# Batch 0 of a fused linear attention and GELU MLP: both transposes first, both kv next, both x in one stretch

## The chip, the cores and the metric

The kernel runs on one core of one Trainium2 chip. The metric is the device time of one execution in microseconds (us), as a median of several runs. Most executions of one kernel lie within about 0.3 us of each other here, so a difference of 0.1 us between two medians means little by itself. What happens inside is read from the profile of one execution, whose times count from the start of its span. PE is the matrix engine TensorE, PEld its weight loads, DVE is VectorE, ACT is ScalarE, POOL is GpSimd, SPq and ACTq are the queues that issue DMAs.

## The reference, cut to what matters

```python
q_s = softmax(q over head_dim)          # 8 batches, 8 heads, 576 positions, 64
k_s = softmax(k over positions)
kv  = einsum('bhsd,bhse->bhde', k_s, v)
x   = einsum('bhsd,bhde->bhse', q_s, kv)      # -> 4608 tokens of 512
out = gelu(x @ w_in) @ w_out                  # 512 -> 2048 -> 512
```

(Shortened: the softmaxes are written out in the original.) The second part is nearly all of the arithmetic. The first part must be done for batch 0 before it can start, and for the other batches it is woven into the second part of the batch before.

## The kernel before

Batch 0 goes through these helpers. `half` 0 is heads 0 to 3, `half` 1 heads 4 to 7. `tp` transposes q, `kv` multiplies exp(k) with v, `x` multiplies transposed q with normalised kv, and `h_phase` is the first matrix multiplication with its GELU.

```python
def kv_norm(b, half=None): ...   # VectorE: reciprocal and multiplication, from PSUM
def tp_mm(b, half): ...          # PE: eight 128x128 transposes into one PSUM tile
def tp_evac(b, half, eng="v"):   # copy of that tile to SBUF
    ...
def x_evac(b, hp, eng="v"): ...  # copy of one x tile, 128x512, to SBUF

def cast_wi(i, w, eng):          # f32 -> bf16 of piece i of w_in
    ...
    if eng == "p":
        for h in range(2):
            nc.gpsimd.tensor_copy(out=o[:, 2 * h:2 * h + 2], in_=w[:, 2 * h:2 * h + 2])
    else:
        for c in range(NDM):
            nc.vector.tensor_copy(out=o[:, c], in_=w[:, c])
```

The order of batch 0, as issued:

```python
    exp_q(0, parts=2); exp_k(0, parts=2)
    norm_q(0, 0, 2)                  # multiplication on GpSimd
    norm_q(0, 1, 2, nc.vector)       # multiplication on VectorE
    tp_mm(0, 0)
    cast_v(0, 0, nc.scalar); cast_v(0, 1, nc.scalar)
    tp_evac(0, 0, "s")
    warm(1)
    cast_v(0, 2, nc.gpsimd); cast_v(0, 3, nc.gpsimd)
    ...
    kv_mm(0, 0); kv_norm(0, 0)
    tp_mm(0, 1); tp_evac(0, 1)
    x_mm(0, 0);  x_evac(0, 0, "s")
    cast_wi_dm(0, wi[0], 0, nc.scalar)
    for dm in range(1, NDM):
        cast_wi_dm(0, wi[0], dm, nc.gpsimd)
    kv_mm(0, 1); kv_norm(0, 1)
    x_evac(0, 1)
    x_mm(0, 1);  x_evac(0, 2, "s"); x_evac(0, 3)
    cast_wi(1, wi[1], "p")           # the second piece of w_in, on GpSimd, in two casts
    table(AF.Gelu)
    h_phase(0, {0: [lambda: cast_wi(2, wi[2], "v")], ...}, groups={0: 2, 4: 4, 8: 4}, ...)
```

(Calls are joined on one line and tile allocations are left out.) The groups of `h_phase` mean: column blocks 0 and 1 of the hidden layer run together, four matmuls each, then block 2, then block 3. Blocks 2 and 3 use the second piece of w_in.

The softmax here doesn't subtract the row's maximum and nothing guards it: scores larger than these inputs give would overflow.

Of the kernel before, what the change touches and what calls it, by code (L numbers as in the profile page):

```python
# [16 lines left out]
def kernel(  # L17
# [16 lines left out]
    nc = tc.nc  # L34
# [7 lines left out]
    NDM = DM // 128  # L42
# [10 lines left out]
    psum_h = ctx.enter_context(tc.tile_pool(name="psum_h", bufs=3, space=bass.MemoryType.PSUM))  # L53
    psum_y = ctx.enter_context(tc.tile_pool(name="psum_y", bufs=2, space=bass.MemoryType.PSUM))
    psum_a = ctx.enter_context(tc.tile_pool(name="psum_a", bufs=1, space=bass.MemoryType.PSUM))
# [100 lines left out]
    def cast_v(b, hp, eng=nc.vector):  # L156
        o = v_aug[b % 2][:, hp, :, 0:D]
        i = st[b]["vf"][:, hp, :].rearrange("p (n d) -> p n d", n=NS)
        if eng is nc.scalar:
            eng.copy(out=o, in_=i)  # L160
        else:
            eng.tensor_copy(out=o, in_=i)  # L162
# [5 lines left out]
    def kv_tiles(b):  # L168


        if b == 0:
            p = [psum_h.tile([128, 512], FP32, tag="h", name="kv")[:, 0:256] for i in range(2)]
            ps = psum_a.tile([128, 4, 256], FP32, tag="a2", name="kv")
            st[b]["kvall"] = ps[:, 0::2]
            p += [ps[:, 0, :], ps[:, 2, :]]
        else:
            ps = psum_a.tile([128, 4, 256], FP32, tag="a2", name="kv")
            st[b]["kvall"] = ps
            p = [ps[:, i, :] for i in place]
        st[b]["kv"] = p  # L180
# [7 lines left out]
    def kv_mm(b, half):  # L188


        if "kv" not in st[b]:
            kv_tiles(b)
        for n in range(NS):
            for i in range(2):
                for hh in range(2):
                    hp = 2 * half + i
                    pr = slice(hh * 64, hh * 64 + 64)
                    c = slice((hh ^ i) * 64, (hh ^ i) * 64 + 64)
                    nc.tensor.matmul(  # L199
                        st[b]["kv"][hp][c, 0:D + 1], ek[b % 2][pr, hp, n, :],  # L200
                        v_aug[b % 2][pr, hp, n, 0:D + 1], start=(n == 0), stop=(n == NS - 1),
                    )

    def kv_norm(b, half=None):

        ps = st[b]["kvall"]
        if half is None:
            parts = [(ps, kvc[b], 4)]
        elif b == 0 and half == 0:
            parts = [(st[b]["kv"][hp].unsqueeze(1), kvc[b][:, hp:hp + 1], 1) for hp in range(2)]  # L210
        elif b == 0:
            parts = [(ps, kvc[b][:, 2:4], 2)]
        else:
            parts = [(ps[:, 1:3] if half == 0 else ps[:, 0::3], kvc[b][:, 2 * half:2 * half + 2], 2)]
        for src, dst, m in parts:
            rec = small.tile([128, 4], FP32, tag="reck")
            nc.vector.reciprocal(rec[:, 0:m], src[:, :, D])
            nc.vector.tensor_tensor(  # L218
                out=dst, in0=src[:, :, 0:D],
                in1=rec[:, 0:m].unsqueeze(2).to_broadcast([128, m, D]), op=ALU.mult,  # L220
            )
# [21 lines left out]
    def tp_mm(b, half):  # L243
        if half == 0:
            st[b]["qT"] = attn_sb.tile([128, J, HP, 128], BF16, tag="qT", name="qT")
        if b == 1 and half == 1:
            ps = psum_a.tile([128, 2, J, 2, 128], BF16, tag="a2", name="tp")[:, 0]
        else:
            pool, tag = (psum_h, "h") if half == 1 else (psum_a, "a")
            ps = pool.tile([128, J, 2, 128], BF16, tag=tag)  # L250
        st[b][f"tp{half}"] = ps
        for i in range(2):
            hp = 2 * half + i
            for j in range(J):
                nc.tensor.transpose(  # L255
                    ps[:, j, i, :],
                    st[b]["eq"][:, j, 2 * hp:2 * hp + 2, :].rearrange("p h d -> p (h d)"),
                    identity,
                )

    def tp_evac(b, half, eng="v"):
        o = st[b]["qT"][:, :, 2 * half:2 * half + 2, :]
        if eng == "v":
            nc.vector.tensor_copy(out=o, in_=st[b][f"tp{half}"])
        else:
            nc.scalar.copy(out=o, in_=st[b][f"tp{half}"])
# [12 lines left out]
    def x_tile(b, hp, pool, tag):  # L279
        if "xT" not in st[b]:  # L280
            st[b]["xT"] = attn_sb.tile([128, HP, M], BF16, tag="xT", name="xT")
        st[b][f"x{hp}"] = pool.tile([128, M], FP32, tag=tag, name="ps")

    def x_mm(b, half):

        for bb in range(B if b == B else 1):
            for r in range(2):
                for i in range(2):
                    hp = 2 * half + i
                    pr = slice(r * 64, r * 64 + 64)  # L290
                    c = slice((r ^ i) * 64, (r ^ i) * 64 + 64)
                    ps = st[b][f"x{hp}"]
                    if b < B:
                        nc.tensor.matmul(  # L294
                            ps[c, :], kvc_of(b, hp)[pr], st[b]["qT"][pr, :, hp, :],
                            start=True, stop=True,
                        )
                    else:
                        nc.tensor.matmul(  # L299
                            ps[c, bb * R:(bb + 1) * R], kvc_of(bb, hp)[pr],  # L300
                            st[b]["qT"][pr, bb // 2, hp, bb % 2 * R:(bb % 2 + 1) * R],
                            start=True, stop=True,
                        )

    def x_all(b):

        for hp in range(HP):
            pool, tag = (psum_h, "h") if hp < 3 else (psum_a, "a")
            x_tile(b, hp, pool, tag)
        x_mm(b, 0)  # L310
        x_mm(b, 1)
        for hp, eng in ((0, "s"), (2, "v"), (1, "s"), (3, "v")):
            x_evac(b, hp, eng)

    def x_evac(b, hp, eng="v"):
        ps = st[b][f"x{hp}"]
        if eng == "v":
            nc.vector.tensor_copy(out=st[b]["xT"][:, hp, :], in_=ps)  # L318
        else:
            nc.scalar.copy(out=st[b]["xT"][:, hp, :], in_=ps)  # L320
# [88 lines left out]
    def load_wi(i):  # L409

        w = wst.tile([128, NDM, 512], FP32, tag="w")
        n = wi_cols[i]
        src = moe_w_in[:, wi_off[i]:wi_off[i] + n].rearrange("(c p) f -> p c f", p=128)
        d = NDM // wi_parts[i]
        for c in range(0, NDM, d):
            nc.sync.dma_start(out=w[:, c:c + d, 0:n], in_=src[:, c:c + d])
        return w
# [15 lines left out]
    def cast_wi_dm(i, w, dm, eng):  # L433

        n = wi_cols[i]
        r = n // 128
        o = wi_bf[:, dm, wi_off[i]:wi_off[i] + n].rearrange("p (c m) -> p c m", c=r)
        w = w[:, dm, 0:n].rearrange("p (m c) -> p c m", c=r)
        if eng is nc.scalar:
            eng.copy(out=o, in_=w)  # L440
        else:
            eng.tensor_copy(out=o, in_=w)

    def load_wo(i):
        w = wst.tile([128, 4, DM], FP32, tag="w")
# [26 lines left out]
    def warm(n, z=zeros):  # L472
        ps = psum_y.tile([128, DM], FP32, tag="y")
        for i in range(n):
            nc.tensor.matmul(ps, z[:, 0:128], z, start=True, stop=True)  # L475
# [12 lines left out]
    wi = [load_wi(i) for i in range(5)]  # L488
# [22 lines left out]
    tp_mm(0, 0)  # L511
    cast_v(0, 0, nc.scalar)
    cast_v(0, 1, nc.scalar)
    tp_evac(0, 0, "s")
    warm(1)
    cast_v(0, 2, nc.gpsimd)
    cast_v(0, 3, nc.gpsimd)
    x_tile(0, 0, psum_y, "y")
    x_tile(0, 1, psum_y, "y")
    kv_mm(0, 0)  # L520
    kv_norm(0, 0)
    tp_mm(0, 1)
    tp_evac(0, 1)
    x_tile(0, 2, psum_a, "a")
    x_mm(0, 0)
    x_evac(0, 0, "s")
    cast_wi_dm(0, wi[0], 0, nc.scalar)
    for dm in range(1, NDM):
        cast_wi_dm(0, wi[0], dm, nc.gpsimd)
    kv_mm(0, 1)  # L530
    kv_norm(0, 1)
    x_evac(0, 1)
    x_tile(0, 3, psum_h, "h")
    x_mm(0, 1)
    x_evac(0, 2, "s")
    x_evac(0, 3)
# [109 lines left out]
    for c in range(2, B + 1):  # L646
# [19 lines left out]
        if c < B:  # L666
            w = [lambda c=c: x_all(c + 1)]
# [34 lines left out]
```

## Time and profile before

| what | before |
|---|---|
| time, median of 3 | 279.65 us (279.54 to 279.83) |
| span of the profiled run | 278.0 us |
| PE busy | 97% of the span |
| first matmul of the hidden layer (line 327) | 14.32 us |
| first matmul of the output layer (line 355) | 28.15 us |

The last two rows are the milestones. They are the first rows of lines 327 and 355 in PE's timeline. From the second milestone to the end of the span, 249.8 us pass (278.0 - 28.15). If this figure is the same in every variant, all that a variant gains or loses lies ahead of the second milestone. The prediction below shows the chain and the rows of the engines.

### The profile page before, as it was taken

The page shows a single profiled execution, that of the slowest core. Times are in us where ns is not written, and L with a number is a line of the kernel's source. Part 1 is how long each engine was busy: PE and PEld are TensorE (multiplying, and loading weights), DVE is VectorE, ACT ScalarE, POOL GpSimd, SP SyncE. Part 2 cuts the span into 40 slices and gives each one's busy share as a digit, 9 for nine tenths or more (in the row PEclk, how much of TensorE's full clock was granted, in tenths as well). Part 3 has the DMA queues.
Part 4 walks back from the last instruction along what each step waited for, and adds up shares of the span by engine and source line. Part 5 has one row for each costly group of instructions (what it writes and reads, how often), then busy time and mean ns, then how long its engine had stood idle before and what let it go on. Part 6 is the DMA issues. An engine that isn't in the chain of part 4 may idle for free.

```text
span 278.0 us, 4534 instructions
## 1 busy us (share of the span) xinstructions
PE 270.0 (97%) x1891; PEld 126.5 (46%) x1919; DVE 100.7 (36%) x153; ACT 158.0 (57%) x247; POOL 32.8 (12%) x26
## 2 busy tenths in 40 slices
PE   7899999999999999999999999999999999999995
PEld 3444454444444444444444444444444444444443
DVE  2876574319743540093008400651015200130012
ACT  4867675789377816791569246943683363136400
POOL 1520051002020220014000500050005000000000
PEclk9999999999999999999999999999999999999999
DMA  7999999963993139702981199017502500220033
GB/s 253 398 386 429 397 402 407 398 257 103 287 348 61 66 79 295 283 38 86 267 329 40 42 247 383 38 51 190 115 0 75 151 2 0 75 78 0 0 78 77
DMA packets 44980, 50.10 MB, mean 180 GB/s; under 512 B 20384, under 2 KB 29856, under 8 KB 44704
## 3 DMA queue, kind: packets, MB, share of 16 engines
q1 hardware_dynamic: 44560, 49.39, 53.5%
q10 hardware_dynamic: 400, 0.43, 0.6%
q8 instruction: 15, 0.25, 0.3%
q14 instruction: 5, 0.04, 0.0%
HBM read 36.70 MB, written 9.44 MB: 166 GB/s over the span
## 4 chain that ended last, share of the span: by engine, by line
PE 94%; DMA 2%; issue 1%; ACT 1%; SPq 1%; DVE 0%
PE ps L327 44%; PE ps L355 43%; DMA f<-in_k_dram 2%; PE kv L199 2%; PE ps L294 2%; PE ps L380 1%; PE pair L327 1%; ACT ek L150 0%; ACT v_aug L160 0%; PE ps L255 0%; SPq L90 0%; PE ps L299 0%; SPq L103 0%; PE tp L255 0%; DVE kvc L218 0%
## 5 line engine op out<-in xcount | busy, mean ns | idle before, releaser
L327 PE MATMUL ps<-xT,wi_bf 128*128 128x512 bf16 x557 | 124.2, 380 | 0.5
L355 PE MATMUL ps<-wo_bf,g 128*128 128x512 bf16 x543 | 122.1, 380 | 1.6 <-issue 1.1
L333 ACT ACTIVATE g<-ps 128x512 bf16<-128x512 f32 x142 | 83.5, 598 | 66.8 <-PE ps L327 66.8
L327 PEld LDWEIGHTS <-wi_bf 128*128 128x128 bf16 x576 | 56.1, 98 | 68.0 <-issue 0.5
L355 PEld LDWEIGHTS <-g 128*128 128x128 bf16 x560 | 53.9, 98 | 64.3 <-issue 0.4
L363 DVE COPY y_sb<-ps 128x512 f32<-128x512 f32 x33 | 22.7, 687 | 81.7 <-PE ps L355 78.6
L238 POOL TENSOR_TENSOR e<-e,recq 128x2048 bf16<-128x2048 bf16 (+1 forms) x9 | 25.7, 2855 | 176.2 <-DVE recq L237 141.5
L162 DVE CAST v_aug<-f 128x576 bf16<-128x576 f32 x24 | 16.4, 746 | 47.5 <-DMA f<-in_v_dram 47.5
L236 DVE TENSOR_REDUCE qsum<-e 128x16 f32<-128x1024 bf16 (+1 forms) x13 | 21.1, 1621 | 14.4 <-ACT e L145 14.3
L320 ACT CAST xT<-ps 128x512 bf16<-128x512 f32 x18 | 9.9, 588 | 28.8 <-PE ps L294 18.8
L145 ACT ACTIVATE e<-f 128x512 bf16<-128x512 f32 (+1 forms) x42 | 20.5, 556 | 3.5 <-DMA f<-in_q_dram 3.5
L150 ACT ACTIVATE ek<-f 128x2304 bf16<-128x2304 f32 (+1 forms) x10 | 17.2, 1728 | 0.5 <-DMA f<-in_k_dram 0.4
L318 DVE CAST xT<-ps 128x512 bf16<-128x512 f32 x17 | 11.0, 686 | 17.0 <-PE ps L294 14.1
L79 ACT ACT_TABLE_LOAD x9 | 11.5, 1283 | 2.8 <-issue 2.6
L475 PE MATMUL ps<-zeros 128*128 128x512 f32 (+1 forms) x15 | 9.2, 773 | 1.5 <-DVE zeros L500 1.5
L145 ACT ACT_TABLE_LOAD x7 | 9.0, 1283 | 0.1
L431 DVE CAST wi_bf<-w 128x512 bf16<-128x512 f32 x12 | 7.3, 654 | 2.2 <-DMA w<-in_moe_w_in_dram 1.9
L199 PEld LDWEIGHTS <-ek 64*64 64x64 bf16 x576 | 6.6, 105 | 2.6 <-ACT wo_bf L470 0.4
L199 PE MATMUL kv<-v_aug,ek 64*64 64x65 bf16 x576 | 7.2, 194 | 0.2 <-ACT v_aug L160 0.2
L294 PE MATMUL ps<-qT,kvc 64*64 64x512 bf16 x62 | 5.7, 391 | 0.8 <-DVE kvc L218 0.6
L238 DVE TENSOR_TENSOR e<-e,recq 128x1024 bf16<-128x1024 bf16 x4 | 6.2, 1546 | 0.1
L475 PEld LDWEIGHTS ps<-zeros 128*128 128x128 f32 x14 | 3.5, 260 | 6.0 <-issue 4.5
(39 smaller groups left out, 49.9 us busy)
## 6 DMA issues: line engine op xcount, KB each, us to landing
out_dram<-y_sb SPq DMA_DIRECT2D x32, 256.0 KB, 2.4
f<-in_k_dram SPq DMA_DIRECT2D x6, 1152.0 KB, 9.7
f<-in_v_dram SPq DMA_DIRECT2D x6, 1152.0 KB, 11.7
f<-in_q_dram SPq DMA_DIRECT2D x6, 1024.0 KB, 7.2
w<-in_moe_w_in_dram SPq DMA_DIRECT2D x6, 512.0 KB, 8.7
f<-in_v_dram SPq DMA_DIRECT2D x8, 288.0 KB, 6.8
f<-in_q_dram SPq DMA_DIRECT2D x4, 512.0 KB, 12.5
w<-in_moe_w_out_dram SPq DMA_DIRECT2D x2, 1024.0 KB, 11.7
```

The source lines that it names most:

```text
L79: nc.scalar.activation(out=scr[:, 1:2], in_=scr[:, 0:1], func=func)
L145: nc.scalar.activation(out=dst[:, i], in_=src[:, u], func=AF.Exp)
L150: nc.scalar.activation(out=ek[b % 2][:, i:i + n], in_=st[b]["kf"][:, i:i + n].rearrange("p x (n d) -> p x n d", n=NS), func=AF.Exp,)
L162: eng.tensor_copy(out=o, in_=i)
L199: nc.tensor.matmul(st[b]["kv"][hp][c, 0:D + 1], ek[b % 2][pr, hp, n, :], v_aug[b % 2][pr, hp, n, 0:D + 1], start=(n == 0), stop=(n == NS - 1),
L236: nc.vector.reduce_sum(out=qsum, in_=eq[:, :, hs, :], axis=AX.X)
L238: eng.tensor_tensor(out=eq[:, :, hs, :], in0=eq[:, :, hs, :], in1=recq.unsqueeze(3).to_broadcast([128, J, w, D]), op=ALU.mult,)
L327: nc.tensor.matmul(ps, wi_bf[:, dm, t * 128:(t + 1) * 128], st[c]["xT"][:, dm, :], start=(dm == 0), stop=(dm == NDM - 1),)
L333: nc.scalar.activation(out=st[c]["g"][:, t, :], in_=ps, func=AF.Gelu)
L355: nc.tensor.matmul(ps, st[c]["g"][:, t, j * 128:(j + 1) * 128], wo_bf[:, t, :], start=(t == 0), stop=(t == NDF - 1),)
L363: nc.vector.tensor_copy(out=y_sb, in_=ps)
L475: nc.tensor.matmul(ps, z[:, 0:128], z, start=True, stop=True)
```

## The change

The intent: let kv of half 1 run directly behind kv of half 0, and both x in one stretch, so that nothing stands between the last piece of v and the hidden layer. The evacuations of the transposes change engines, because VectorE is idle at the first one and busy with the normalisation of kv at the second. ScalarE is relieved of a cast.

```diff
     tp_mm(0, 0)
     cast_v(0, 0, nc.scalar)
     cast_v(0, 1, nc.scalar)
-    tp_evac(0, 0, "s")
-    warm(1)
+    tp_evac(0, 0)
     ...
+    tp_mm(0, 1)
+    tp_evac(0, 1, "s")
+    x_tile(0, 2, psum_a, "a")
     kv_mm(0, 0)
     kv_norm(0, 0)
-    tp_mm(0, 1)
-    tp_evac(0, 1)
-    x_tile(0, 2, psum_a, "a")
+    kv_mm(0, 1)
+    kv_norm(0, 1)
+    for dm in range(NDM):
+        cast_wi_dm(0, wi[0], dm, nc.gpsimd)
+    x_tile(0, 3, psum_h, "h")
     x_mm(0, 0)
     x_evac(0, 0, "s")
-    cast_wi_dm(0, wi[0], 0, nc.scalar)
-    for dm in range(1, NDM):
-        cast_wi_dm(0, wi[0], dm, nc.gpsimd)
-    kv_mm(0, 1)
-    kv_norm(0, 1)
     x_evac(0, 1)
-    x_tile(0, 3, psum_h, "h")
     x_mm(0, 1)
```

(The branch for ScalarE in `cast_wi_dm` also goes.)

More of the change, by code (lines that the diff above doesn't have):

```diff
@@ L438, in cast_wi_dm @@
         w = w[:, dm, 0:n].rearrange("p (m c) -> p c m", c=r)
-        if eng is nc.scalar:
-            eng.copy(out=o, in_=w)
-        else:
-            eng.tensor_copy(out=o, in_=w)
+        eng.tensor_copy(out=o, in_=w)
     def load_wo(i):
```

## The prediction

> **What bounds the kernel now.** I read the page first, then the chain of waits over the first 40 us, then each engine's timeline from 9.5 to 18.5 us. The page says the chain is 94% PE, and the list of who waited for whom on PE says that from 14 us to the end there is only one kind of wait left, 1.1 us of it under "issue":
>
> ```profile
> PE 94%; DMA 2%; issue 1%; ACT 1%; SPq 1%; DVE 0%
> PE ps L355 <- issue: 1.1, 7, 0.2
> ```
>
> So from the first matmul of the first hidden layer (line 327) onward, PE is the bound, back to back. The change touches only what comes before it. What can be won is the start of that stream, and it can only be kept if nothing behind it (a cast, a DMA) is then late. The chain before the stream:
>
> ```profile
> 2.34 6.62 DMA f<-in_k_dram
> 8.96 0.02 issue
> 8.98 1.16 ACT ek L150
> 10.15 1.15 ACT v_aug L160 x2
> 11.29 0.04 issue
> 11.33 0.47 PE kv L199 x34
> 11.81 0.55 PE ps L255 x8
> 12.36 0.52 PE ps L294 x2
> 12.88 0.53 PE kv L199 x31
> 13.41 0.02 issue
> 13.43 0.18 DVE rec L217
> ...
> 13.64 0.30 DVE kvc L218
> ...
> 13.98 0.41 PE ps L294 x4
> ```
>
> Columns: start, length, what. K lands at 8.96, ScalarE makes exp(k) and casts two pieces of v (to 11.29), PE does kv of half 0 and then, one after the other, the second transposes, the first x, kv of half 1; VectorE normalises; the second x ends the stretch at 14.39. (The timeline shows the line-327 stream starting at 14.32, overlapping that x.) Between 11.81 and 12.88 kv of half 1 stands in line behind transposes and x, though its last input is ready earlier. That is seen in GpSimd's timeline, with the wait before each row in brackets, and VectorE's:
>
> ```profile
> 11.18 1.38 POOL L162 CAST v_aug<-f 128x576 bf16<-128x576 f32 x2 [1.29 <-DMA f<-in_v_dram]
> 13.31 1.12 POOL L442 CAST wi_bf<-w 128x256 bf16<-128x256 f32 x3 [0.75 <-DMA w<-in_moe_w_in_dram]
> 14.66 1.23 POOL L428 CAST wi_bf<-w 128x512 bf16<-128x512 f32 x2 [0.23 <-DMA w<-in_moe_w_in_dram]
> 15.32 1.04 DVE L431 CAST wi_bf<-w 128x512 bf16<-128x512 f32 x1 [0.16 <-DMA w<-in_moe_w_in_dram]
> 12.52 0.68 DVE L264 COPY qT<-ps 128x1024 bf16<-128x1024 bf16 x1
> 11.19 1.00 ACT L266 COPY qT<-ps 128x1024 bf16<-128x1024 bf16 x1
> ```
>
> V's last piece is cast by 12.56 (11.18 + 1.38). So kv of half 1 could run from 12.6 instead of 12.88: about 0.28 us of order, not of work. That is what the change is after.
>
> **What the Trainium skill says.** "TensorE: Matmul & The Clock Gate", section Back-to-back issue gap, gives N/2.4 + 2.5 ns, 216 ns at N = 512; the chain near the end has 15 of line 355 in 3.24 us, 216 ns each, so it agrees and I use 0.216. "VectorE: DVE Perf Modes", section The TRN2 errata, gives PSUM to SBUF costs of 120 + FD/Accel cycles at 0.96 GHz for VectorE and 172 + FD/Accel at 1.2 GHz for ScalarE; for the transposes (1024 bf16, two at a time on VectorE) that is 0.66 and 1.00 us, and the trace has 0.68 and 1.00. "SBUF — State Buffer", section Who interferes with whom, says that a VectorE cast in a two-port mode and a GpSimd instruction exclude each other: whoever starts first keeps the shared ports for the whole instruction. The trace agrees: the VectorE cast at 15.32 took 1.04 us, where the median of its twelve is 0.62, and GpSimd's second cast of line 428 (15.25, 0.64 long) was running. I use this below.
>
> **The change part by part.**
>
> 1. Second transposes before kv of half 0. They need the second half of q normalised by VectorE, which the timeline shows from 9.46 to 10.98. The first eight transposes end at 10.76. The second eight then run from about 11.03, start to start 0.056, last start 11.42. The extra warm-up matmul that filled this gap (10.60, 0.38 us) is gone; it was on no one's path. Kv of half 0 waited until 11.33 for ScalarE's v cast; now it comes after the transposes, about 11.57, and ends 0.5 later, 12.1 instead of 11.81. That is a loss of 0.25 us, but on a path with slack (step 3).
>
> 2. Evacuations swapped. VectorE takes the first transposes at about 10.95, to 11.63, when it sat idle anyway (it waited 0.86 us before the first reciprocal). ScalarE takes the second, 11.68 to 12.68. Both are done before their x needs them.
>
> 3. Kv of half 1 directly behind kv of half 0. VectorE's normalisation of half 0 took from 11.84 to 12.60, 0.76 us; it now runs 12.12 to 12.88. Kv of half 1 waits for v's last cast (12.56 plus 0.04) and takes 0.5 us as half 0 did: end 13.11, against 13.37. Its normalisation took 0.50 (13.43 to 13.93): now 13.15 to 13.65.
>
> 4. Both x in one stretch. X of half 0 runs in the shadow of that normalisation, 12.95 to 13.35; ScalarE evacuates it in 0.59, to 13.98. X of half 1 starts at about 13.70 instead of 13.98. In the trace the stream started 0.34 after x did (13.98 to 14.32), so now at 14.04. The first evacuation is ready at about 14.02, just in time. **Gain: 14.32 - 14.04 = 0.28 us.**
>
> 5. The first w_in cast off ScalarE. ScalarE loses 0.42 us it had between two evacuations, worth nothing: its next instruction waited for PE until 14.44. GpSimd gets a fourth cast. Start to start is 0.36 us, so they run 13.31 to about 14.79; the stream wants them at 14.04, 14.47, 14.90, 15.33 and they are ready at 13.72, 14.08, 14.43, 14.79. No wait. But line 428's two casts move from 14.66 to about 14.73 for the first and from 15.25 to about 15.32 for the second.
>
> The rest of the stream has slack above 0.28 where I looked: the last cast of w_in ends at 24.67 and is wanted at about 25.0 after the shift; the first of w_out ends at 27.35 and is wanted at 27.87. The Gelu table load comes behind ScalarE's last evacuation and moves with it. So without step 5's consequence: 279.65 - 0.28 = 279.37.
>
> **Rivals.**
>
> A. GpSimd's second cast of line 428 loses the ports. Its start moves to 15.32, exactly the time at which VectorE's first cast of the next piece is released by its DMA. If VectorE starts first, it takes 0.62, to 15.94, and GpSimd's cast ends about 0.5 later, at about 16.45. The third block of columns needs it at its third matmul, 14.04 + 8 x 0.216 + 2 x 0.216 = 16.20. PE would wait about 0.3 us and the whole gain would be gone: about 279.65. For it: the two starts coincide within what I can work out, and VectorE is idle and waiting while GpSimd is still finishing its first cast until 15.37. Against it: 0.05 us of DMA landing decides it. I give it 55%.
>
> B. PE's clock. The removed warm-up matmul and a PE that idles from 12.1 to 12.6 could bring a lower granted clock. The page shows the clock at 9 tenths or more in every slice, although the kernel before idles as much (10.98 to 11.33, 13.4 to 13.98). A few us at a lower clock would cost over 1 us: above 280.5. 4%.
>
> C. DMA hides or eats the gain: the weights come at their own pace (the DMA share is 1.0 and more from 4 to 28 us). The casts above keep at least 0.3 us of slack, so I expect nothing before A. Were w_in later than read here, the result is again 279.65.
>
> **Range and chances.** 0.45 x 279.37 + 0.55 x 279.65 is 279.52; I say 279.5. The three runs of before spread over 0.29 us, so a median can be off by 0.1 or more, and each of steps 3 and 4 by 0.1. Range 279.1 to 279.9. Two per cent is 5.6 us, twenty times what is at stake: within 2% is 0.98, each side 0.01.
>
> **What would show it.** Step 1: second transposes at 11.0, kv of half 0 ending at 12.1. Step 3: kv of half 1 ending at 13.1, released by the GpSimd v cast. Step 4: the first line-327 matmul at 14.04 instead of 14.32. Step 5 and A: four GpSimd casts from 13.3; then either the second line-428 cast takes 0.64 and the VectorE cast beside it about 1.1, or the VectorE cast takes 0.62 and the line-428 one over 1.0, with a PE wait for it at 16.2. The prediction is wrong if PE's clock falls, if ScalarE's evacuation of the first x holds the stream, or if PE gets a new wait after 16.5.

## The result, and the profile after

The changed kernel takes 279.68 us (median of 6 runs, 279.55 to 279.75), the kernel before 279.63 us in the same rounds. The ratio is 1.0001, with a 95% interval from 0.9988 to 1.0014: the same time. (Ratios are the mean time of one kernel's fast runs over that of the other's fast runs of the same rounds, so not quite the ratio of the medians.)

That nothing changed in the total does not mean that nothing happened. PE's timeline of the changed kernel; the columns are start, length, engine, line, operation, and in brackets the wait before the row:

```profile
11.03 0.61 PE L255 MATMUL ps<-identity,e 128*128 128x128 bf16 x8 [0.55 <-DVE e L238]
11.57 0.55 PE L199 MATMUL kv<-v_aug,ek 64*64 64x65 bf16 x38
12.64 0.48 PE L199 MATMUL kv<-v_aug,ek 64*64 64x65 bf16 x34 [0.52 <-POOL v_aug L162]
12.93 0.40 PE L294 MATMUL ps<-qT,kvc 64*64 64x512 bf16 x4
13.71 0.41 PE L294 MATMUL ps<-qT,kvc 64*64 64x512 bf16 x4 [0.38 <-DVE kvc L218]
14.06 6.23 PE L327 MATMUL ps<-xT,wi_bf 128*128 128x512 bf16 x27
28.11 1.24 PE L355 MATMUL ps<-wo_bf,g 128*128 128x512 bf16 x5
```

The hidden layer starts at 14.06 instead of 14.32, 0.26 us earlier, and the rows ahead of it are in the new order, with kv of half 1 waiting for nothing but GpSimd's cast of v. But the output layer starts at 28.11 instead of 28.15: of 0.26 us, 0.04 are left. Between the milestones 14.05 us pass, where the kernel before took 13.83. The chain of waits says what took the 0.22:

```profile
6.91 6.36 DMA w<-in_moe_w_in_dram
13.27 0.05 issue
13.32 1.48 POOL wi_bf L439 x4
14.80 1.59 POOL wi_bf L428 x2
16.40 0.05 issue
16.45 0.60 PE ps L327 x2
```

The chain that sets the end no longer runs through k, kv and x at all. It runs through GpSimd: four casts of the first piece of w_in, two of the second, and then a matmul at 16.45 that waited for the last of them. The engines' timelines show why the last one is late:

```profile
15.25 0.62 DVE L431 CAST wi_bf<-w 128x512 bf16<-128x512 f32 x1 [0.36 <-DMA w<-in_moe_w_in_dram]
15.34 1.05 POOL L428 CAST wi_bf<-w 128x512 bf16<-128x512 f32 x1
```

VectorE's cast started 0.09 us ahead of GpSimd's and took its ordinary 0.62 us. GpSimd's took 1.05 us instead of 0.64. In the kernel before (rows in the prediction) GpSimd's started 0.07 us ahead of VectorE's, and the 1.04 us were VectorE's, where nobody waited for them.

### The profile page after: what moved, and what is told of

The parts are those of the page before. It is cut to its first block, busy times and chain, and to the rows that moved or that the text cites. A ratio compares the mean times of both kernels' runs of the same rounds, so it can differ in the third digit from the quotient of the medians.

```text
span 277.9 us, 4563 instructions
## 1 busy us (share of the span) xinstructions
PE 271.6 (98%) x1918; PEld 126.1 (45%) x1918; DVE 100.6 (36%) x153; ACT 157.9 (57%) x246; POOL 33.4 (12%) x27
## 4 chain that ended last, share of the span: by engine, by line
PE 93%; DMA 4%; POOL 1%; ACTq 0%; SPq 0%; issue 0%; DVE 0%
PE ps L355 44%; PE ps L327 43%; DMA w<-in_moe_w_in_dram 2%; DMA touch<-in_moe_w_in_dram 2%; PE kv L199 2%; PE ps L294 1%; PE ps L380 1%; PE pair L327 1%; POOL wi_bf L428 1%; POOL wi_bf L439 1%; PE ps L299 0%; PE tp L255 0%; ACTq L482 0%; PE ps L255 0%; ACTq L101 0%; SPq L103 0%
## 5 line engine op out<-in xcount | busy, mean ns | idle before, releaser
L355 PE MATMUL ps<-wo_bf,g 128*128 128x512 bf16 x560 | 124.2, 379 | 0.0
L472 PE MATMUL ps<-zeros 128*128 128x512 f32 x14 | 8.6, 779 | 1.4 <-DVE zeros L497 1.4
```

Source lines behind the costliest of these rows:

```text
L355: nc.tensor.matmul(ps, st[c]["g"][:, t, j * 128:(j + 1) * 128], wo_bf[:, t, :], start=(t == 0), stop=(t == NDF - 1),)
L472: nc.tensor.matmul(ps, z[:, 0:128], z, start=True, stop=True)
```

## The experiments

Twelve runs were made, of eleven new kernels and of the changed kernel once more, each with 5 rounds or more, in three sets beside the kernel before. Its median was 279.65 us in each set. All gave correct results. The theory is the **ports theory**: the earlier start is given back in a wait for a GpSimd cast that has lost the shared ports to VectorE. Its first rival is that an earlier start is absorbed in any case, by DMA or by something later.

All milestones, from the profiled run of each kernel, with the time of that one execution and the median of all. (Where an edit added lines above them, the two lines are numbered 328 and 356 or 331 and 359.)

| kernel | line 327 starts | line 355 starts | between | this execution us | median us |
|---|---|---|---|---|---|
| before | 14.32 | 28.15 | 13.83 | 279.74 | 279.65 |
| changed | 14.06 | 28.11 | 14.05 | 279.73 | 279.68 |
| e1_act_cast | 14.45 | 28.27 | 13.82 | 279.87 | 279.85 |
| e2_pool_cast_only | 14.24 | 28.06 | 13.82 | 279.65 | 279.65 |
| e3_dve_late | 14.28 | 28.09 | 13.81 | 279.68 | 279.49 |
| e4_dve_half | 14.07 | 27.88 | 13.81 | 279.47 | 279.51 |
| e5_after_again | 14.14 | 27.95 | 13.81 | 279.57 | 279.61 |
| e6_kv_first | 13.76 | 27.58 | 13.82 | 279.20 | 279.28 |
| e7_dve_half_qlate | 14.21 | 28.04 | 13.83 | 279.62 | 279.62 |
| e8_kv_first_qlate | 14.14 | 27.96 | 13.82 | 279.54 | 279.30 |
| e9_before_dve_half | 14.21 | 28.03 | 13.82 | 279.62 | 279.62 |
| e10_dve_half_qlate1 | 14.90 | 28.71 | 13.81 | 280.32 | 280.16 |
| e11_kv_first_qlate1 | 14.16 | 27.98 | 13.82 | 279.61 | 279.66 |
| e12_kv_first_pool | 13.96 | 28.03 | 14.07 | 279.60 | 279.60 |

A milestone is that of one execution, the median that of five or six, so these two need not agree to 0.1 us: in e3 and e8 the profiled execution was the slowest of five. From line 355 to the end of the span, 249.8 us pass in e6 (277.4 - 27.58) as in e10 (278.5 - 28.71), in the changed kernel (277.9 - 28.11) and in the one before. In all fourteen profiles the time of the execution is 251.57 to 251.63 us more than the start of line 355. Over a range of more than 1 us, what is won or lost ahead of line 355 goes through to the end one to one. The rival that it is absorbed later falls with this.

### e1: the first cast back on ScalarE

```diff
+    cast_wi_dm(0, wi[0], 0, nc.scalar)      # behind x_evac(0, 0, "s")
-    for dm in range(NDM):
+    for dm in range(1, NDM):
         cast_wi_dm(0, wi[0], dm, nc.gpsimd)
```

> The changed kernel with one part undone: the first w_in cast back on ScalarE, behind its evacuation of the first x; the new order stays. Ports theory (the gain of 0.26 us at the stream's start was taken back by the second line-428 cast waiting for VectorE): GpSimd has three casts, its second cast of 128x512 starts near 15.25 again and may win or lose; the ScalarE cast (13.95 to 14.37) now holds the stream's first matmul to about 14.40 instead of 14.06. Stream starts 14.35 to 14.45, no wait at its third column block; time 279.65 to 279.75. Rival (the changed order itself gains nothing, something later absorbs it): the same time too, but with the stream at 14.06.

The stream started at 14.45, at the edge of what was expected, and nothing waited in the third column block (13.82 us between the milestones). The time, 279.85 us, is 0.1 above the expectation. With the new order ScalarE's cast stands directly ahead of the hidden layer, and the first matmul waited for it, so in this place it could not stay.

### e2: the cast move alone

```diff
     x_evac(0, 0, "s")
-    cast_wi_dm(0, wi[0], 0, nc.scalar)
-    for dm in range(1, NDM):
+    for dm in range(NDM):
         cast_wi_dm(0, wi[0], dm, nc.gpsimd)
```

> The kernel before with one part alone: the first w_in cast on GpSimd, order and evacuations as before. Ports theory: stream starts at 14.32 as before, GpSimd's second 128x512 cast moves to about 15.33 and loses the ports to VectorE's cast at 15.25 to 15.3, so it ends about 16.4; it is wanted at 14.32 + 10 x 0.216 = 16.48, so no wait of PE: time 279.65, same as before within 0.1. If PE is held by more than 0.1 us there, time 279.75 or more.

Met. VectorE's cast started at 15.15, GpSimd's at 15.21, 0.06 later, and GpSimd's took 1.07 us, to 16.28. In the old order it is wanted at 14.24 + 10 x 0.216 = 16.40 in this run, so nobody waited, and the time is 279.65 us. The lost ports cost nothing by themselves: they cost where the stream is early enough to want the cast.

### e3: more work for VectorE

```diff
     cast_wi(1, wi[1], "p")
+    for i in range(2):
+        nc.vector.memset(delay, 0.0)        # scratch, 128x512 f32, read by nobody
```

> The changed kernel with work added: two VectorE memsets of a scratch tile (about 0.5 us each, nobody reads it) ahead of VectorE's first w_in cast, so that GpSimd's second 128x512 cast starts first and has the ports. Ports theory: that GpSimd cast takes 0.64 instead of 1.05 us, ends by 16.0, PE has no wait in the third column block, the first line-355 matmul starts 0.2 us earlier than in the changed kernel and the span falls by 0.2: time 279.4 to 279.5, although 1 us of work was added. Rival (DMA or a later cast absorbs any earlier start): VectorE's later casts come late or PE waits elsewhere, time 279.65 or more.

Between the milestones 13.81 us pass instead of 14.05, though an engine was given 1 us of useless work. GpSimd's row of this run:

```profile
15.31 0.64 POOL L429 CAST wi_bf<-w 128x512 bf16<-128x512 f32 x1
```

The memset kept VectorE's cast away until 16.08, GpSimd's cast had the ports and took 0.64. That shows why the cast had been long. The missing wait shows nothing yet: in this execution the stream itself started late, at 14.28, so the cast was wanted at 14.28 + 10 x 0.216 = 16.44, and even one of 1.05 us would have ended in time, at 16.36. For the same reason line 355 started at 28.09, not 0.2 earlier as expected. The median fell to 279.49 us; the profiled execution, at 279.68, was the slowest. The chain of this run says why the stream was late:

```profile
13.07 0.59 PE ps L295 x4
13.65 0.58 ACT xT L321
14.24 0.04 issue
14.28 0.81 PE ps L328 x3
```

The stream waited for ScalarE's evacuation of the first x, not for the second x. Hence the **theory of a second chain**: in the new order kv of half 0 stands behind the second transposes, and these wait for VectorE's normalisation of q. (The profile names ScalarE's cast of v as what released these transposes in e1, e3, e4 and e5; but they start 0.15 us after the end of VectorE's multiplication of q there, as in the changed kernel and e10, and they read nothing of v.) So the arrival of q, its normalisation, the transposes, kv of half 0, its normalisation, the first x and its evacuation are now a chain that ends just where the one through v ends. In this run ScalarE's exp of q started at 5.25, in the changed kernel's profile at 4.97.

### e4: the second half of the cast on VectorE

```diff
-            for h in range(2):
-                nc.gpsimd.tensor_copy(out=o[:, 2 * h:2 * h + 2], in_=w[:, 2 * h:2 * h + 2])
+            nc.gpsimd.tensor_copy(out=o[:, 0:2], in_=w[:, 0:2])
+            nc.vector.tensor_copy(out=o[:, 2:4], in_=w[:, 2:4])
```

> The changed kernel with the second half of the second w_in piece cast by VectorE instead of GpSimd. Ports theory: the VectorE cast starts about 14.9, waits for GpSimd's first one to give up the ports (15.39) and ends about 15.9, before it is wanted at 16.2; no PE wait, gain of 0.2 to 0.26 kept: time 279.4 to 279.5. Rival (absorbed later): 279.65.

Met: stream at 14.07, no wait, line 355 at 27.88, 279.51 us, ratio to before 0.9995 (0.9983 to 1.0008). This is the clean pair for the wait: the stream started where that of the changed kernel did (14.06), and its eleventh matmul at 16.22 instead of 16.45. In its profile line 355 is 0.27 us earlier than in the kernel before, so what was gained at the start arrives whole. Its stream too was released by ScalarE's evacuation, although v was early here (GpSimd's casts of v ended at 12.27):

```profile
10.88 1.39 POOL L162 CAST v_aug<-f 128x576 bf16<-128x576 f32 x2 [1.00 <-DMA f<-in_v_dram]
14.07 0.81 PE L327 MATMUL ps<-xT,wi_bf 128*128 128x512 bf16 x3 [0.26 <-ACT xT L320]
```

### e5: the changed kernel again

> The changed kernel once more, unaltered, beside the next three. Ports theory: whatever the start of the stream (14.0 to 14.3, it follows the arrival of q and v), VectorE's first w_in cast takes 0.62 and GpSimd's second 128x512 cast about 1.05 us, and from the stream's start to the first line-355 matmul 14.05 us pass instead of the 13.82 of the kernel before. Time 279.6 to 279.75.

Half a miss. GpSimd's cast lost again (15.02 to 16.08, 1.06 us, VectorE ahead by 0.07), but PE did not wait for it: in this execution w_in came earlier (GpSimd's first piece started at 13.02 instead of 13.32), and the stream started at 14.14, so the cast was wanted only at 16.30. The time is 279.61 us. The profile names a GpSimd cast as what released that first matmul, but ScalarE's evacuation (13.50, 0.59 long) ended within 0.05 us of it, so this row alone does not say which it was. The spacing settles it: the stream started 2.96 us after the first of the second transposes, exactly as in e3, e4 and e10, where the evacuation released it. So this was the second chain, in the changed kernel itself; v alone (cast by 12.28) would have allowed about 13.75. The wait is what is left over of an early start: the stream cannot pass the end of the late cast, and where something has held the stream already, no wait is seen.

### e6: kv of half 0 back ahead of the second transposes

```diff
 # on top of e4
-    tp_mm(0, 1)
-    tp_evac(0, 1, "s")
-    x_tile(0, 2, psum_a, "a")
     kv_mm(0, 0)
     kv_norm(0, 0)
+    tp_mm(0, 1)
+    tp_evac(0, 1, "s")
+    x_tile(0, 2, psum_a, "a")
     kv_mm(0, 1)
```

> The kernel with the VectorE half cast (e4), and kv of half 0 put back ahead of the second transposes; the rest of the new order stays. Theory of a second chain (in the new order q's arrival, its VectorE normalisation, second transposes, kv 0, first x, ScalarE's evacuation have come to set the stream's start along with v): kv of half 0 ends at 11.8 instead of 12.1, the first x is free earlier, stream starts at 13.9 to 14.05, 13.8 us to the first line-355 matmul; time 279.35 to 279.5. Rival (v's last cast alone sets the start): no earlier than e4, 279.5.

More than met: 279.28 us, ratio 0.9992 (0.9979 to 1.0004). Its chain:

```profile
11.13 0.47 PE kv L199 x34
11.60 0.55 PE ps L255 x8
12.16 0.15 PE kv L199 x2
12.30 0.04 issue
12.35 0.50 PE kv L199 x34
...
13.42 0.41 PE ps L294 x4
13.83 3.34 PE ps L327 x15
```

Kv of half 0 is done before the transposes need PE, and the stream starts behind the second x again, at 13.76. GpSimd's casts of v ended at 12.29 here, as in e4 (12.27) and e5 (12.28), whose streams started at 14.07 and 14.14. With the same arrival of v, the second chain cost 0.3 to 0.4 us. One rule fits all these profiles: the stream starts 1.46 to 1.47 us after the end of v's last cast (the changed kernel, e6, e7, e8, e11, e12), or, with kv of half 0 behind the second transposes, 2.96 us after these begin (e3, e4, e5, e10), whichever is later: for instance 12.59 and 14.06 in the changed kernel, 11.11 and 14.07 in e4.

### e7 and e8: q made late, the first attempt

```diff
 # e7 on top of e4, e8 on top of e6
+    nc.vector.memset(delay, 0.0)            # 0.5 us, batch 0
     norm_q(0, 1, 2, nc.vector)
```

> e4 with a VectorE memset of 0.5 us of a scratch tile ahead of the second half of q's normalisation, which delays the second transposes by 0.5. Theory of a second chain: all of kv 0, its normalisation, the first x and its evacuation move, the stream starts at 14.4 to 14.5 instead of 14.07; time 279.85 to 279.95. Rival (v's cast alone sets the start, q has slack): 14.07 and 279.5.

> e6 with the same 0.5 us memset. Theory of a second chain: kv of half 0 no longer stands behind the second transposes, these have slack up to v's last cast (12.6), so the delay of 0.5 costs at most 0.1: stream at 13.95 to 14.15, time 279.4 to 279.55, well below e7. Rival: as e7.

E7 missed, and tells nothing of the second chain: 279.62 us, with q's second half multiplied by 10.95, as early as in e4 (10.96). The memset of 0.48 us was swallowed. VectorE's multiplication started later (9.72), overlapped GpSimd's multiplication of the first half by only 0.12 us, and took 1.23 us; in e4 it started at 9.31, overlapped by 0.57, and took 1.65. So e7 is in effect a second sample of e4, and e8 (279.30 us, below its expected 279.4 to 279.55; ratio 0.9988, 0.9974 to 1.0001) a second sample of e6. V was late in both profiles (GpSimd's casts ended at 12.75 and 12.68), and both streams were then set by v, at 14.21 and 14.14.

### e9: e4's edit on the kernel before

The edit is that of e4, applied to the kernel before.

> Control: the kernel before, with only the VectorE half cast of e4. In the kernel before GpSimd's second 128x512 cast was never waited for by PE, so ports theory: stream start and the 13.82 us to the first line-355 matmul unchanged, time 279.65 within 0.1. Rival (the half cast is a gain of its own): 279.4.

Met: 279.62 us, ratio 1.0001. Where PE never waited for the GpSimd cast, taking half of it away is worth nothing.

### e10 and e11: q made late, where nothing swallows it

```diff
 # in norm_q, for the second half of batch 0 only; e10 on top of e4, e11 on top of e6
         nc.vector.reciprocal(recq, qsum)
+        for _ in range(2):
+            nc.vector.memset(delay, 0.0)    # 2 x 0.5 us
         eng.tensor_tensor(...)
```

> e4 with two memsets of a scratch tile (0.5 us each) between the reciprocal and the multiplication of q's second half, where nothing can swallow them, as it did in e7. The multiplication gets quicker once GpSimd's is done (1.23 instead of about 1.6), so the second transposes come some 0.7 us late, at 11.7. Theory of a second chain: the stream starts at 14.7 to 14.9, 13.82 to the first line-355 matmul, time 280.1 to 280.3. Rival: q has slack, 279.5 to 279.6.

> e6 with the same two memsets. Theory of a second chain: kv of half 0 is no longer behind the transposes; their ScalarE evacuation then ends near 13.4 and the first x's near 14.1: stream at 14.0 to 14.3, time 279.4 to 279.7, 0.5 us or more below e10. Rival: as e10.

Both met: 280.16 us (six runs, one of them 281.27) and 279.66 us. With the order of the changed kernel the stream slipped to 14.90, along this chain:

```profile
10.23 0.48 DVE delay L241
10.72 1.09 DVE e L242
...
11.94 0.61 PE ps L259 x8
12.55 0.90 PE kv L200 x72
...
13.49 0.79 PE ps L298 x4
14.28 0.58 ACT xT L324
...
14.90 2.10 PE ps L331 x9
```

This is the second chain, link by link, from q's normalisation to the stream. With kv of half 0 ahead of the transposes the same delay left the stream at 14.16. Some of what e11 lost against e6 came from another side: VectorE's delayed multiplication now ran beside GpSimd's cast of v, and the two v casts took 1.82 us together instead of 1.38.

### e12: e6 without the half cast

The edit is that of e6, applied to the changed kernel.

> The changed kernel with kv of half 0 ahead of the second transposes, and w_in's second piece cast by GpSimd as in the changed kernel (e6 without the VectorE half). Ports theory: the stream starts as early as in e6, but VectorE's first w_in cast keeps the ports, GpSimd's second 128x512 cast takes 1.05 us, to 16.1 to 16.4, and PE waits for it 0.3 to 0.5 us: an earlier start only lengthens the wait, time 279.55 to 279.7. Rival (e6's gain came from the order alone): 279.3.

Met in the time: the stream started at 13.96, earlier than in the changed kernel though later than in e6 (v was cast by 12.50 instead of 12.29), and line 355 at 28.03. Its chain and rows repeat the picture:

```profile
13.24 1.48 POOL wi_bf L439 x4
14.71 1.60 POOL wi_bf L428 x2
...
16.36 0.82 PE ps L327 x3
```

Between the milestones 14.07 us pass: the earlier start became a wait of about 0.25, a little less than the 0.3 to 0.5 expected. The time is 279.60 us. So e6's gain needs both edits: e3, e4 and e7, which lift the ports alone, have 279.49, 279.51 and 279.62; e12, which lifts the second chain alone, has 279.60; with both lifted, e6 and e8 have 279.28 and 279.30.

E6 is the best version: 0.37 us under the kernel before in its set, 0.13%. Two samples of it agree, but two of the five runs of e6 (279.63 and 279.73) are no faster than the kernel before, and the interval of each just reaches 1.0; that it is faster rests on the two samples together and on the milestones.

## Why the prediction was right or wrong

The prediction was right: 279.5 was said, with 279.1 to 279.9, and 279.68 was measured. The number proves little, as the range holds both the full gain and none. The mechanism is the better test: rival A was seen as described in one of the two profiles of the changed kernel. In the other, e5, what the prediction named as a sign of being wrong came true, that "ScalarE's evacuation of the first x holds the stream". That the time was right there too was luck.

- **What bounds.** PE from line 327 on. Shown: 249.8 us from line 355 to the end in every variant. Its 0.216 us for a matmul is measured; the page gives the formula cited with it for an isolated matmul (see the last section).
- **Step 1.** Second transposes at 11.03, kv of half 0 from 11.57 and ended at about 12.1, as said (a loss of 0.29 by these figures, where it says 0.25). That this loss lies "on a path with slack" was the weak point: in the changed kernel's profile ScalarE's evacuation of the first x ended at 13.95 and the stream started at 14.06, so the slack was under 0.1 us, and there was none in e3, e4, e5 and e10. Its own step 4 left 0.02 (the evacuation ready at 14.02, the stream at 14.04): two chains that end together, each moving by tenths from execution to execution with the arrival of q and v. The working takes both arrivals as fixed.
- **Step 2.** VectorE evacuated the first transposes from 10.81, ScalarE the second from 11.68 in 1.01 us, as worked out.
- **Step 3.** Kv of half 1 was released by GpSimd's v cast, and its normalisation ended at 13.66, said 13.65.
- **Step 4.** Line 327 at 14.06, said 14.04. The gain of 0.28 was 0.26, between the two executions profiled. Over more profiles it is smaller. With all ahead of the stream as in the changed kernel it started at 14.06, 14.28, 14.07 and 14.14 (changed, e3, e4, e5), in the old order at 14.32, 14.24 and 14.21 (before, e2, e9): means of 14.14 and 14.26, so an estimate of 0.12 from seven executions.
- **Step 5 and rival A.** This came out, to 0.1 us: GpSimd's cast was said to end at 16.45 and ended at 16.39, PE was said to wait 0.3 and waited 0.23 (a matmul at 16.45 whose place in the stream was 14.06 + 10 x 0.216 = 16.22). It was given 55%; it happened in the profile of the changed kernel, and GpSimd lost the ports in all four profiles in which it had all four first-piece casts and both second-piece casts with no added work on VectorE (the changed kernel, e2, e5, e12).
- **Rival B.** PE's clock stayed at 9 tenths or more in every slice. The removed warm-up matmul cost nothing visible.
- **Rival C.** Not seen: no later cast was waited for, even in e6 with its stream at 13.76.

So why was an order that was better by 0.26 us in one execution worth nothing in the end? Because two things that had slack before lost it together. One is the second w_in piece on GpSimd, moved later by the added cast and wanted earlier by the stream, so that losing the ports by 0.09 us mattered. The other is q, which the new order put on the path. Lifting either alone gave at most 0.16 us (e3), lifting both 0.37. How often the changed kernel loses its gain in the one way and how often in the other is left open: there are two profiles of it, one with the wait (the first) and one with the late start (e5).

## What to carry to other kernels

When an engine's start is moved earlier, list what it will want and when, including the things that were never waited for before, and move their deadlines by the same amount. Work that is moved to an idle engine shifts everything behind it on that engine; check what those shifted instructions will now collide with. Putting one group of work ahead of another to straighten the path also puts the inputs of the first group on the path: here a reorder with the half that had to wait for v alone was better than one that also waited for q.

## What the Trainium skill lacked or had wrong

- "SBUF — State Buffer", section Who interferes with whom, has the mechanism right: the first to start keeps the shared ports. It gives no figure for a close race. Here a lead of 0.06 to 0.09 us in the recorded starts (those of GpSimd are rough) went with the win each time (VectorE ahead in the changed kernel, e2, e5 and e12, GpSimd ahead by 0.07 before), and the loser's cast took 1.04 to 1.07 us instead of 0.62 to 0.64. The loss is smaller than the overlap: GpSimd's cast started 0.53 us before VectorE's ended and lost 0.41.
- The same section says that a VectorE instruction with two SBUF inputs contends with GpSimd's reads. The runs agree and add the size: VectorE's multiplication of 128x1024 took 1.58 us where it overlapped GpSimd's own multiplication by 0.51 us (the changed kernel), and 1.23 where by 0.12 (e7); GpSimd's two v casts took 1.82 us beside it in e11 instead of 1.38.
- "TensorE: Matmul & The Clock Gate", section Back-to-back issue gap, calls the formula that the prediction cites the gap of an isolated matmul, and gives about 131 ns for each matmul of a sustained stream at N = 512. Here a stream of 15 took 216 ns each, so it is the formula that fits.
- No page has the spread of DMA arrivals between executions of one program. In these profiles ScalarE's first exp of q, which waits for its DMA, started between 4.97 us (changed) and 5.37 us (e10), more than the whole effect under study.
